# A decode block on one core: value cache loaded as one 32 KB packet per partition, the last quarter of w_down in three pieces, four stores on one semaphore

## The chip, the cores and the metric

The kernel runs on one core of a Trainium2 chip. A core has a matrix engine (TensorE, PE in the profile, with its weight loads shown as PEld), a vector engine (VectorE, DVE), a scalar engine (ScalarE, ACT), a general engine (GpSimd, POOL) and a sync engine (SyncE, SP) that here only issues loads. Sixteen DMA engines move data between the chip's memory (HBM) and the on-chip memory (SBUF, 128 partitions); matmul results go to PSUM, eight banks of 512 float32 per partition. The engines run side by side and wait for one another on semaphores. The metric is the device time of one execution in microseconds; the time before is the median of three runs.

## The reference

One step of a transformer block with conditioning: eight sequences (B = 8), one new token each, a width of 1024, 32 query heads on 4 key/value heads of 128, and a cache of 8192 positions per sequence and head, everything in bfloat16.

```python
mod = (silu(c) @ w_mod).reshape(8, 6, 1, -1)          # sa, ca, ga, sb, cb, gb
h = layernorm(x) * (1 + ca) + sa
q = (h @ wq) as 32 heads of 128
p = softmax(q . k_cache * 128 ** -0.5)                # 8 queries share a key/value head
x = x + ga * ((p . v_cache) @ wo)
h = layernorm(x) * (1 + cb) + sb
gate, up = h @ W_gate, h @ W_up                       # 1024 -> 3584
x = x + gb * ((relu(gate) * up) @ W_down)             # 3584 -> 1024
```

The two caches are 64 MiB each; the weights are some 50 MB. Each byte of them is needed once.

## The kernel before

**Writing order and waits.** Every operation is recorded in one list per engine (`_Graph`); a helper works out which operation must wait for which, and one semaphore per engine counts the operations that somebody waits for. So nearly all instructions carry the line of a helper: 366 for matmuls (`mm`), 370 for transposes on TensorE (`tr`), 374 for VectorE (`dve`), 377 for ScalarE (`act`), 684 for the loads on SP, 87 for the small transfers. The pair loop is emitted as a hardware loop on TensorE, VectorE and ScalarE: one turn is two pairs, and the waits in it are on values that grow with the turn.

**Loads.** All loads go through SP in one order (`stream`, lines 291 to 328), into a ring of five slots of 32 KB per partition, A to E. A load waits until the last user of what lay there before is done (lines 682 to 687). The order is w_mod in two halves, wq in two halves, keys of pair 0, then for each pair n the keys of pair n + 1 and the values of pair n, wo's first half after the values of pair 0, wo's second half, w_gate and w_up in halves, and w_down. Keys alternate between slots A and B, values between C and D. Each key or value load is 4 MiB.

**A pair.** Pair n is one sequence and two of its four key/value heads (16 pairs). The keys come as 128 rows per partition, 32 KB in one piece: partitions 0 to 63 hold the first head's rows, 64 to 127 the second's. The values come in two pieces of 16 KB per partition, one per head, each partition holding 64 rows of each head (line 309).

- `slot_keys(n, j)`, 16 slots per pair: eight 128x128 transposes of keys into one of three PSUM banks taken in turn (`t_bank`), copied out by VectorE (even slots) or ScalarE (odd). Line 507 picks the key rows so that the order of the keys in the scores agrees with that of the values.
- `slot_scores`: for each two slots, four matmuls with a stationary of 32 columns and 512 moving columns, on the four column groups of the array; the scores of a pair fill two banks of 128 partitions.
- `soft_max` to `soft_exp`: the maximum per partition, brought together over partitions with two small matmuls, and one `Exp` on ScalarE that writes P, 128 x 1024, and its row sums.
- `turn_p(n, h)`: P is turned with four 128x128 transposes for each half h, and the copies into `pt` (VectorE for h = 0, ScalarE for h = 1) put the columns in the order in which the values are used.
- `pv(n, u)`, u = 0 to 7: four matmuls, on the four column groups, with 32 columns of `pt` stationary and 512 columns of values moving; all eight steps add up in bank 7 (`W`).
- `pv_evac`, `o_sum`, `o_evac`: the 128 x 512 sums are multiplied with a mask (`diag`) that keeps a quarter of them, summed over four groups, added over partitions with a matmul (`sel`) which also adds the row sums, divided, and put in place for the output projection.

These stages are interleaved over pairs (lines 590 to 628): while slot j of pair n is turned, pair n - 1 gets its maximum (j = 2), exponent (6), turn of P (8) and value products (9 to 15), and pair n - 2 its output (0 to 3).

**Before and after the loop.** POOL fills constants and two identities; VectorE derives masks from them (`spread`, lines 394 to 404) and clears five banks. Then come the transposes of x and silu(c), the products with w_mod, the first layernorm, and q. After the loop: wo, the second layernorm, gate and up, and w_down (lines 659 to 671): four quarters of seven row groups, four matmuls of 256 columns for each. The first two quarters are one load, the third is one, and the last comes as six row groups and one. Two VectorE operations make the output rows; four stores of 4 KB, two on SP and two on ScalarE's queue, each have a semaphore (`osem`), and SP waits for all four at the end.

Of the kernel before, what the change touches and what calls it, by code (L numbers as in the profile page):

```python
# [11 lines left out]
class _Op:  # L12
    __slots__ = ("eng", "fn", "deps", "inc", "value", "idx", "sem", "semval")

    def __init__(self, eng, fn, idx):
        self.eng = eng
        self.fn = fn
        self.deps = []
        self.inc = False
        self.value = 0  # L20
        self.idx = idx
        self.sem = None
        self.semval = 0


# [160 lines left out]
def bass_adaLN_cond__gqa_block_cached__glu_gated_reglu__decode_kernel(  # L186
# [24 lines left out]
    NP = B * G // 2  # L211
# [8 lines left out]
    with ExitStack() as es:  # L220
# [29 lines left out]
        P = sb("P", [128, 1024], bf16)  # L250
        pt = sb("pt", [128, 1024], bf16)
        ov = sb("ov", [128, 512], f32)
        od = sb("od", [128, 132], f32)
        rl = sb("rl", [128, 1], f32)
        tm = sb("tm", [128, 128], f32)
        sel = sb("sel", [128, 128], f32)
        sel16 = sb("sel16", [128, 16], f32)
        diag = sb("diag", [128, 4, 128], bf16)
        blk = sb("blk", [128, 8, 16], f32)
# [17 lines left out]
        xsem = E(nc.semaphore("d_x"))  # L277
        osem = [E(nc.semaphore("d_o%d" % i)) for i in range(4)]

# [73 lines left out]
        loads["v", -1] = loads["wq", 0]  # L353
        place["v", -1] = ring[:, D_:D_ + SLOT].rearrange("p (a n) -> p a n", a=2)

# [37 lines left out]

        def spread(view, n, tile, key):
            dve("tensor_reduce", sel16[:, 0:n], view, AX.X, ALU.add, reads=["identf"], writes=["sel16"])
# [5 lines left out]
        dve("tensor_reduce", sel16[:, 0:4], identf[:].rearrange("p (q i r) -> p i q r", q=4, i=4), AX.XY, ALU.add, reads=["identf"], writes=["sel16"])  # L401
        dve("tensor_copy", diag[:], sel16[:, 0:4, None].to_broadcast([128, 4, 128]), reads=["sel16"], writes=["diag"])
        spread(identf[:].rearrange("p (y k) -> p k y", k=8), 8, blk, "blk")
# [137 lines left out]
        def soft_exp(n):  # L541
            act(P[:].rearrange("p (i k a) -> p i a k", k=64, a=2), S(n).rearrange("p h (i a k) -> p (h i) a k", i=4, a=2), ACT.Exp,
                bias=nb[:], scale=SCALE, accum_out=od[:, 128:129], reads=[pS(n, 0), pS(n, 1), "nb"], writes=["P", "od1"])

        def turn_p(n, h):
            t = t_bank()
            for i in range(4):
                tr(TB(t)[:, 128 * i:128 * (i + 1)], P[:, 512 * h + 128 * i:512 * h + 128 * (i + 1)], identb[:], ["P", "identb"], [pT[t]])
            to = pt[:, 512 * h:512 * (h + 1)].rearrange("p (r i h) -> p i r h", r=16, i=4)
            of_ = TB(t)[:, 0:512].rearrange("p (i r h) -> p i r h", i=4, r=16)  # L550
            if h == 0:
                dve("tensor_copy", to, of_, reads=[pT[t]], writes=[("pt", 0)])
            else:
                act(to, of_, ACT.Copy, reads=[pT[t]], writes=[("pt", 1)])

        def pv(n, u):
            h, jj = u // 4, u % 4
            for q2 in range(2):
                j = 8 * h + 2 * jj + q2
                for gl in range(2):  # L560
                    q = 2 * gl + q2
                    at = 512 * h + 32 * (8 * gl + 4 * q2 + jj)
                    mm(W[32 * q:32 * (q + 1), :], pt[:, at:at + 32],
                       place[("v", n)][:, gl, 512 * j:512 * (j + 1)], u == 0, u == 7, [("pt", h)], [pW], ("v", n))

        def pv_evac(n):
            dve("tensor_tensor", out=ov[:], in0=W, in1=diag[:].rearrange("p i d -> p (i d)"), op=ALU.mult, reads=[pW, "diag"], writes=["ov"])
            dve("tensor_reduce", od[:, 0:128], ov[:].rearrange("p (i d) -> p d i", i=4), AX.X, ALU.add, reads=["ov"], writes=["od"])
# [90 lines left out]
        for c_ in range(4):  # L659
            for i in range(7):  # L660
                if c_ < 2:
                    key, w = ("wd", 0), place[("wd", 0)][:, c_, i, :]
                elif c_ == 2:
                    key, w = ("wd", 1), place[("wd", 1)][:, i, :]
                elif i < 6:
                    key, w = ("wd", 2), place[("wd", 2)][:, i, :]
                else:
                    key, w = ("wd", 3), place[("wd", 3)][:, 0, :]
                for q in range(4):
# [3 lines left out]
        dve("tensor_tensor", out=outR[:], in0=fR, in1=x1R[:], op=ALU.add, reads=["ov", "x1R"], writes=["outR"])  # L673
        last = []
        for q in range(4):
            o = g.dma("sp" if q % 2 == 0 else "act", out.rearrange("b o d -> (b o) d")[:, 256 * q:256 * (q + 1)], outR[32 * q:32 * q + B, :],
                      osem[q], 16, reads=["outR"])
            last.append(o)

# [48 lines left out]
```

## Time and profile before

| | |
|---|---|
| median of three runs | 440.71 us (440.56 to 440.88) |
| the profiled execution | 440.41 us, of which the span of the profile is 438.2 us |
| TensorE busy | 307.3 us, 70% of the span |
| VectorE, ScalarE busy | 184.2 us and 180.5 us, 42% and 41% |
| moved by DMA | 185.81 MB, 424 GB/s over the span |
| granted TensorE clock, mean | 0.895 |

The profile is one execution on the chip. A page gives busy times, queues and the costliest groups; views of the trace give the chain of work that ended last, instructions in order of time with what ended the idle time before them, and busy times by stage. Times are in microseconds from the start of the span unless marked ns. A line of the timeline has the start, the duration from the first to the last of the instructions in it, engine, line, operation, output and inputs, shapes, the count, and in brackets the idle time before it and its releaser. The trace also has a record of every DMA packet, with its start, duration, size and queue, though not its DMA engine; where the text speaks of one engine's packets, these records were strung together by size and time.

### The profile page before, as it was taken

The numbers are of one execution on the slowest core, as the hardware profiler recorded it, in microseconds if no ns is written. First come the engines' busy times: TensorE is split into PE (matmuls) and PEld (weight loads), VectorE is DVE, ScalarE is ACT, GpSimd is POOL, SyncE is SP. The second block draws the span as 40 slices with busy tenths as digits, with TensorE's granted clock in tenths as the row PEclk, the third lists the DMA queues.
The fourth block names the chain that finished last, engine by engine and source line by source line (L and its number), as shares of the span: only waits on it lengthen the run. The fifth ranks groups of instructions, "written<-read, shape, count | busy, mean of one in ns | idle before, by whom it ended". The sixth has DMA issues, their size and how long they took to land.

```text
span 438.2 us, 9770 instructions
## 1 busy us (share of the span) xinstructions
PE 307.3 (70%) x3999; PEld 185.4 (42%) x3999; DVE 184.2 (42%) x358; ACT 180.5 (41%) x197; POOL 9.4 (2%) x48
## 2 busy tenths in 40 slices
PE   1415458896978888696777879677787979656063
PEld 1102135554554655354454545445454655232031
DVE  4102046635372654636264554627355464431010
ACT  3000017463654646464473646456464646300000
POOL 3000000000000000000000000000000000000000
PEclk9968669996999799999999989999998899885666
DMA  8999999999999999999999999999999999999994
GB/s 362 431 431 432 443 432 408 449 429 424 419 450 414 447 419 449 420 438 434 426 438 425 437 425 437 429 431 441 425 440 429 447 416 449 421 429 439 419 431 199
DMA packets 8908, 185.81 MB, mean 424 GB/s; under 512 B 785, under 2 KB 817, under 8 KB 961
## 3 DMA queue, kind: packets, MB, share of 16 engines
q1 hardware_dynamic: 8832, 185.61, 98.6%
q8 instruction: 9, 0.15, 0.1%
q10 hardware_dynamic: 64, 0.04, 0.0%
q14 instruction: 3, 0.02, 0.0%
HBM read 185.63 MB, written 0.02 MB: 424 GB/s over the span
## 4 chain that ended last, share of the span: by engine, by line
DMA 61%; PE 21%; issue 8%; DVE 6%; ACT 2%; DVEq 0%; SPq 0%; ACTq 0%
DMA ring<-in_A_k_cache_dram 45%; PE PS L370 11%; PE PS L366 10%; DMA ring<-in_B_W_up_dram 6%; DMA ring<-in_B_W_down_dram 6%; DMA ring<-in_w_mod_dram 4%; ACT KT L377 2%; DVE KT L374 2%; DVE ov L374 1%; DVE tm L374 1%; DVE nm L374 1%; ACT P L377 0%; DVE nb L374 0%; DVE rl L374 0%; DVEq L161 0%
## 5 line engine op out<-in xcount | busy, mean ns | idle before, releaser
L377 ACT ACTIVATE KT<-PS 128x1024 bf16<-128x1024 bf16 (+1 forms) x132 | 132.9, 1008 | 173.2 <-PE PS L370 85.5
L370 PE MATMUL PS<-identb,ring 128*128 128x128 bf16 x2048 | 159.9, 226 | 27.4 <-DMA ring<-in_A_k_cache_dram 27.4
L370 PEld LDWEIGHTS PS<-identb,ring 128*128 128x128 bf16 x2048 | 122.7, 101 | 83.1 <-issue 66.4
L374 DVE COPY KT<-PS 128x1024 bf16<-128x1024 bf16 (+1 forms) x130 | 89.5, 689 | 162.0 <-PE PS L370 118.9
L366 PE MATMUL PS<-KT,Z 128*32 128x512 bf16 x516 | 53.6, 403 | 0.2 <-ACT KT L377 0.2
L366 PE MATMUL PS<-ring,pt 128*32 128x512 bf16 x544 | 49.6, 384 | 0.2 <-DVE pt L374 0.2
L377 ACT ACT_TABLE_LOAD x11 | 14.1, 1283 | 32.0 <-PE PS L370 30.3
L377 ACT ACTIVATE P<-PS,nb 128x1024 bf16<-128x1024 f32 x17 | 24.0, 1410 | 6.3 <-DVE nb L374 4.8
L366 PE MATMUL PS<-od,sel 128*128 128x129 f32 x36 | 10.2, 369 | 18.2 <-DVE od L374 18.2
L366 PE MATMUL PS<-ring,h2T 128*8 128x512 bf16 (+1 forms) x128 | 11.9, 548 | 13.4 <-DMA ring<-in_B_W_up_dram 9.9
L374 DVE TENSOR_REDUCE mp<-PS 128x1 f32<-128x1024 f32 x17 | 20.6, 1213 | 0.0
L366 PEld LDWEIGHTS PS<-KT,Z 128*32 128x32 bf16 x516 | 13.4, 93 | 14.9 <-issue 1.6
L366 PE MATMUL PS<-ring,siluT 128*8 128x512 bf16 x96 | 9.3, 560 | 14.6 <-DMA ring<-in_w_mod_dram 14.6
L370 PE MATMUL PS<-identb,P 128*128 128x128 bf16 x136 | 13.7, 227 | 7.2 <-ACT KT L377 7.1
L374 DVE TENSOR_REDUCE od<-ov 128x128 f32<-128x512 f32 x18 | 18.4, 1021 | 0.6
L366 PEld LDWEIGHTS PS<-ring,pt 128*32 128x32 bf16 x544 | 14.2, 95 | 7.9 <-issue 0.6
L366 PEld LDWEIGHTS PS<-od,sel 128*128 128x128 f32 x36 | 6.3, 220 | 22.2 <-DVE od L374 22.2
L366 PE MATMUL PS<-ring,hT 128*8 128x512 bf16 x64 | 6.9, 606 | 10.6 <-DMA ring<-in_A_wq_dram 10.6
L377 ACT ACTIVATE pt<-PS 128x512 bf16<-128x512 bf16 x17 | 10.1, 597 | 9.9 <-PE PS L370 9.9
L374 DVE TENSOR_TENSOR ov<-PS,diag 128x512 f32<-128x512 f32 x18 | 12.3, 682 | 3.1 <-PE PS L366 3.1
L370 PEld LDWEIGHTS PS<-identb,P 128*128 128x128 bf16 x136 | 8.0, 100 | 12.5 <-ACT KT L377 9.9
L366 PEld LDWEIGHTS PS<-ring,h2T 128*8 128x8 bf16 x128 | 3.8, 118 | 21.1 <-DMA ring<-in_B_W_up_dram 11.5
(84 smaller groups left out, 128.7 us busy)
## 6 DMA issues: line engine op xcount, KB each, us to landing
ring<-in_A_k_cache_dram SPq DMA_DIRECT2D x16, 4096.0 KB, 22.0
ring<-in_A_v_cache_dram SPq DMA_DIRECT2D x16, 4096.0 KB, 30.8
ring<-in_w_mod_dram SPq DMA_DIRECT2D x2, 6144.0 KB, 24.1
ring<-in_A_wq_dram SPq DMA_DIRECT2D x2, 4096.0 KB, 46.0
ring<-in_A_wo_dram SPq DMA_DIRECT2D x2, 4096.0 KB, 32.3
ring<-in_B_W_gate_dram SPq DMA_DIRECT2D x2, 3584.0 KB, 25.0
ring<-in_B_W_up_dram SPq DMA_DIRECT2D x2, 3584.0 KB, 31.5
ring<-in_B_W_down_dram SPq DMA_DIRECT2D x1, 3584.0 KB, 37.3
```

Source lines behind the costliest of these rows:

```text
L366: return pe(lambda e: e.matmul(out_, lhsT, rhs, start=start, stop=stop, skip_group_check=True), reads, writes, block, deps)
L370: return pe(lambda e: e.matmul(out_, in_, ident, start=True, stop=True, is_transpose=True), reads, writes, block)
L374: return g.op("dve", lambda e: getattr(e, name)(*args, **kw), reads, writes)
L377: return g.op("act", lambda e: e.activation(*args, **kw), reads, writes)
```

## The change

Three parts.

1. **Values.** A value load takes 128 consecutive rows per partition, as the keys do, so that each partition receives 32 KB of one head in one piece. Partitions 0 to 63 hold the first head's rows, 64 to 127 the second's. What follows from it: the keys need no reordering in `slot_keys`, and `soft_exp` writes P in plain order. In `turn_p`, P is turned by 32 transposes of 64x64 for both halves together, the first head's block in partitions 0 to 63 and the second's in 64 to 127, and the result is copied into a `pt` twice as wide in two copies per half, one per head, so that for each head the other head's partitions stay zero (`pt` is filled with zeros on POOL at the start). `pv` has 16 steps of four matmuls of 256 columns instead of 8 steps of four of 512. `pv_evac` works on 256 columns, and `o_sum` uses a new mask `selo` for the output and the old `sel` for the row sums: two matmuls instead of one. A new function `early` moves the waits of the transposes of P onto the operation ahead of them on TensorE, which in the loop is the last key transpose of slot 8.
2. **w_down.** The last quarter comes as four, two and one row groups.
3. **Stores.** The four stores count on one semaphore, and SP waits once, for 64.

```diff
-        osem = [E(nc.semaphore("d_o%d" % i)) for i in range(4)]
+        osem = E(nc.semaphore("d_o"))
...
-            block(("v", n), (C_, D_)[n % 2], SLOT, A_v_cache[b, 2 * gp:2 * gp + 2].rearrange("g (p c) d -> p g (c d)", p=128), (2, 64 * Dh), "v%d" % (n % 2))
+            block(("v", n), (C_, D_)[n % 2], SLOT, A_v_cache[b].rearrange("g s d -> (g s) d")[2 * gp * Sk:2 * (gp + 1) * Sk, :].rearrange("(p c) d -> p c d", p=128),
+                  (128, Dh), "v%d" % (n % 2))
...
-        block(("wd", 2), B_ + 7 * D, 6 * D, wd[:, 3, 0:6], (6, D))
-        block(("wd", 3), B_ + 13 * D, D, wd[:, 3, 6:7], (1, D))
+        block(("wd", 2), B_ + 7 * D, 4 * D, wd[:, 3, 0:4], (4, D))
+        block(("wd", 3), B_ + 11 * D, 2 * D, wd[:, 3, 4:6], (2, D))
+        block(("wd", 4), B_ + 13 * D, D, wd[:, 3, 6:7], (1, D))
...
-                        (Z[:], 0.0, ("Z", 0)), (od[:], 1.0, "od"), (KT[:, 6, :], 0.0, ("KT", 6)), (KT[:, 7, :], 0.0, ("KT", 7))):
+                        (Z[:], 0.0, ("Z", 0)), (pt[:], 0.0, "pt"), (od[:], 1.0, "od"), (KT[:, 6, :], 0.0, ("KT", 6)), (KT[:, 7, :], 0.0, ("KT", 7))):
...
+        spread(identf[:].rearrange("p (q g i h) -> p g h q i", q=4, g=2, i=2), 16, selo, "selo", AX.XY)
+        spread(identf[:].rearrange("p (q i r) -> p i q r", q=8, i=2), 2, diag, "diag", AX.XY)
...
-                cc = 64 * (e_ % 2) + 4 * j + e_ // 2
-                tr(TB(t)[:, 128 * e_:128 * (e_ + 1)], place[("k", n)][:, cc, :], identb[:], ["identb"], [pT[t]], ("k", n))
+                tr(TB(t)[:, 128 * e_:128 * (e_ + 1)], place[("k", n)][:, 8 * j + e_, :], identb[:], ["identb"], [pT[t]], ("k", n))
...
-            act(P[:].rearrange("p (i k a) -> p i a k", k=64, a=2), S(n).rearrange("p h (i a k) -> p (h i) a k", i=4, a=2), ACT.Exp,
+            act(P[:], S(n).rearrange("p h c -> p (h c)"), ACT.Exp,
                 bias=nb[:], scale=SCALE, accum_out=od[:, 128:129], reads=[pS(n, 0), pS(n, 1), "nb"], writes=["P", "od1"])
+
+        def early(at):
+            ops = g.prog["pe"]
+            while ops[at - 1].apart:
+                at -= 1
+            for o in ops[at:]:
+                o.apart = True
+                ops[at - 1].deps.extend(o.deps)
+                o.deps = []
 
         def turn_p(n, h):
             t = t_bank()
-            for i in range(4):
-                tr(TB(t)[:, 128 * i:128 * (i + 1)], P[:, 512 * h + 128 * i:512 * h + 128 * (i + 1)], identb[:], ["P", "identb"], [pT[t]])
...
+            at = len(g.prog["pe"])
+            for i in range(8):
+                for gl in range(2):
+                    r = slice(64 * gl, 64 * (gl + 1))
+                    tr(TB(t)[r, 64 * i:64 * (i + 1)], P[r, 512 * h + 64 * i:512 * h + 64 * (i + 1)], identb[r, r], ["P", "identb"], [pT[t]])
+            if n + 1 < NP:
+                early(at)
+
+            for gl in range(2):
+                r = slice(64 * gl, 64 * (gl + 1))
+                to = pt[r, 1024 * h:1024 * (h + 1)].rearrange("p (x g c) -> p g x c", g=2, c=16)[:, gl]
+                of_ = TB(t)[r, 0:512].rearrange("p (x c) -> p x c", c=16)
+                if h == 0:
+                    dve("tensor_copy", to, of_, reads=[pT[t]], writes=[("pt", h, gl)])
+                else:
+                    act(to, of_, ACT.Copy, reads=[pT[t]], writes=[("pt", h, gl)])
 
         def pv(n, u):
...
+            v = place[("v", n)].rearrange("p (h j q e) d -> p h q e j d", h=2, j=4, q=2)
+            for t in (2 * u, 2 * u + 1):
+                for q in range(4):
+                    at = 32 * (4 * t + q)
+                    mm(W[32 * q:32 * (q + 1), 0:256], pt[:, at:at + 32], v[:, t // 8, q // 2, t % 8, 2 * (q % 2):2 * (q % 2) + 2, :],
+                       t == 0, t == 15, [("pt", t // 8, 0), ("pt", t // 8, 1)], [pW], ("v", n))
 
         def pv_evac(n):
...
+            dve("tensor_tensor", out=ov[:, 0:256], in0=W[:, 0:256], in1=diag[:].rearrange("p i d -> p (i d)"), op=ALU.mult, reads=[pW, "diag"], writes=["ov"])
+            dve("tensor_reduce", od[:, 0:128], ov[:, 0:256].rearrange("p (i d) -> p d i", i=2), AX.X, ALU.add, reads=["ov"], writes=["od"])
 
         def o_sum(n):
-            mm(W[:, 0:129], sel[:], od[:, 0:129], True, True, ["sel", "od", "od1"], [pW])
+            mm(W[:, 0:128], selo[:], od[:, 0:128], True, True, ["selo", "od"], [pW])
+            mm(W[:, 128:129], sel[:], od[:, 128:129], True, True, ["sel", "od1"], [pW])
...
-                for o in last:
-                    e.wait_ge(o.sem, o.semval)
+                e.wait_ge(osem, 64)
```

More of the change, by code (lines that the diff above doesn't have):

```diff
@@ L12 @@
 class _Op:
-    __slots__ = ("eng", "fn", "deps", "inc", "value", "idx", "sem", "semval")
+    __slots__ = ("eng", "fn", "deps", "inc", "value", "idx", "sem", "semval", "apart")
     def __init__(self, eng, fn, idx):
@@ L23, in __init__ @@
         self.semval = 0
+        self.apart = False
 class _Buf:
@@ L250, in bass_adaLN_cond__gqa_block_cached__glu_gated_reglu__decode_kernel @@
         P = sb("P", [128, 1024], bf16)
-        pt = sb("pt", [128, 1024], bf16)
-        ov = sb("ov", [128, 512], f32)
+        pt = sb("pt", [128, 2048], bf16)
+        ov = sb("ov", [128, 256], f32)
         od = sb("od", [128, 132], f32)
@@ L256, in bass_adaLN_cond__gqa_block_cached__glu_gated_reglu__decode_kernel @@
         sel = sb("sel", [128, 128], f32)
+        selo = sb("selo", [128, 128], f32)
         sel16 = sb("sel16", [128, 16], f32)
-        diag = sb("diag", [128, 4, 128], bf16)
+        diag = sb("diag", [128, 2, 128], bf16)
         blk = sb("blk", [128, 8, 16], f32)
@@ L353, in bass_adaLN_cond__gqa_block_cached__glu_gated_reglu__decode_kernel @@
         loads["v", -1] = loads["wq", 0]
-        place["v", -1] = ring[:, D_:D_ + SLOT].rearrange("p (a n) -> p a n", a=2)
+        place["v", -1] = ring[:, D_:D_ + SLOT].rearrange("p (c d) -> p c d", d=Dh)
         def pe(fn, reads=(), writes=(), block=None, deps=()):
@@ L391, in bass_adaLN_cond__gqa_block_cached__glu_gated_reglu__decode_kernel, with spread @@
                                                 pattern=[[-1, 128]], channel_multiplier=1), reads=[k], writes=[k])
-        def spread(view, n, tile, key):
-            dve("tensor_reduce", sel16[:, 0:n], view, AX.X, ALU.add, reads=["identf"], writes=["sel16"])
+        def spread(view, n, tile, key, axes=AX.X):
+            dve("tensor_reduce", sel16[:, 0:n], view, axes, ALU.add, reads=["identf"], writes=["sel16"])
             dve("tensor_copy", tile[:].rearrange("p (a z) -> p a z", a=n) if len(tile.shape) == 2 else tile[:],
@@ L400, in bass_adaLN_cond__gqa_block_cached__glu_gated_reglu__decode_kernel @@
         spread(identf[:].rearrange("p (g y h) -> p g h y", g=2, y=8), 16, sel, "sel")
-        dve("tensor_reduce", sel16[:, 0:4], identf[:].rearrange("p (q i r) -> p i q r", q=4, i=4), AX.XY, ALU.add, reads=["identf"], writes=["sel16"])
-        dve("tensor_copy", diag[:], sel16[:, 0:4, None].to_broadcast([128, 4, 128]), reads=["sel16"], writes=["diag"])
+        spread(identf[:].rearrange("p (q g i h) -> p g h q i", q=4, g=2, i=2), 16, selo, "selo", AX.XY)
+        spread(identf[:].rearrange("p (q i r) -> p i q r", q=8, i=2), 2, diag, "diag", AX.XY)
         spread(identf[:].rearrange("p (y k) -> p k y", k=8), 8, blk, "blk")
@@ L545, in turn_p @@
         def turn_p(n, h):
             t = t_bank()
-            for i in range(4):
-                tr(TB(t)[:, 128 * i:128 * (i + 1)], P[:, 512 * h + 128 * i:512 * h + 128 * (i + 1)], identb[:], ["P", "identb"], [pT[t]])
[L549 to L554, printed above, removed]
@@ L556, in pv @@
-        def pv(n, u):
[L557 to L564, printed above, removed]
+            at = len(g.prog["pe"])
[3 more added lines that the diff above has]
+                    tr(TB(t)[r, 64 * i:64 * (i + 1)], P[r, 512 * h + 64 * i:512 * h + 64 * (i + 1)], identb[r, r], ["P", "identb"], [pT[t]])
@@ L566, in pv_evac @@
+        def pv(n, u):
+            v = place[("v", n)].rearrange("p (h j q e) d -> p h q e j d", h=2, j=4, q=2)
[4 more added lines that the diff above has]
+                       t == 0, t == 15, [("pt", t // 8, 0), ("pt", t // 8, 1)], [pW], ("v", n))
         def pv_evac(n):
-            dve("tensor_tensor", out=ov[:], in0=W, in1=diag[:].rearrange("p i d -> p (i d)"), op=ALU.mult, reads=[pW, "diag"], writes=["ov"])
@@ L568, in pv_evac @@
-            dve("tensor_reduce", od[:, 0:128], ov[:].rearrange("p (i d) -> p d i", i=4), AX.X, ALU.add, reads=["ov"], writes=["od"])
+            dve("tensor_tensor", out=ov[:, 0:256], in0=W[:, 0:256], in1=diag[:].rearrange("p i d -> p (i d)"), op=ALU.mult, reads=[pW, "diag"], writes=["ov"])
+            dve("tensor_reduce", od[:, 0:128], ov[:, 0:256].rearrange("p (i d) -> p d i", i=2), AX.X, ALU.add, reads=["ov"], writes=["od"])
         def o_sum(n):
-            mm(W[:, 0:129], sel[:], od[:, 0:129], True, True, ["sel", "od", "od1"], [pW])
+            mm(W[:, 0:128], selo[:], od[:, 0:128], True, True, ["selo", "od"], [pW])
@@ L664, in bass_adaLN_cond__gqa_block_cached__glu_gated_reglu__decode_kernel @@
                     key, w = ("wd", 1), place[("wd", 1)][:, i, :]
-                elif i < 6:
-                    key, w = ("wd", 2), place[("wd", 2)][:, i, :]
-                else:
-                    key, w = ("wd", 3), place[("wd", 3)][:, 0, :]
+                else:
+                    u = 2 + (i >= 4) + (i >= 6)
+                    key, w = ("wd", u), place[("wd", u)][:, i - (0, 4, 6)[u - 2], :]
                 for q in range(4):
@@ L673, in bass_adaLN_cond__gqa_block_cached__glu_gated_reglu__decode_kernel @@
         dve("tensor_tensor", out=outR[:], in0=fR, in1=x1R[:], op=ALU.add, reads=["ov", "x1R"], writes=["outR"])
-        last = []
         for q in range(4):
-            o = g.dma("sp" if q % 2 == 0 else "act", out.rearrange("b o d -> (b o) d")[:, 256 * q:256 * (q + 1)], outR[32 * q:32 * q + B, :],
-                      osem[q], 16, reads=["outR"])
-            last.append(o)
+            g.dma("sp" if q % 2 == 0 else "act", out.rearrange("b o d -> (b o) d")[:, 256 * q:256 * (q + 1)], outR[32 * q:32 * q + B, :],
+                  osem, 16 * (q + 1), reads=["outR"])
         head = []
```

## The prediction

> **What bounds the kernel now.** I read the queues first, then the stages, then the chain of waits, then the timeline of one pair and of the end. From the page's queues and the table of windows (busy time of PE, PEld, DVE, ACT, POOL; granted clock, DMA share, GB/s):
>
> ```profile
> q1 hardware_dynamic: 8832, 185.61, 98.6%
> q8 instruction: 9, 0.15, 0.1%
> ...
> 97.00:370.60 273.60, 220.97 (x2893) 140.27 (x2894) 138.19 (x253) 149.53 (x161) 4.61 (x27) 0.96 1.01 432
> 370.60:433.20 62.60, 31.65 (x423) 14.84 (x419) 12.77 (x32) 5.56 (x8) 0.51 (x2) 0.71 0.99 424
> 433.20:438.20 5.00, 1.67 (x28) 0.81 (x28) 0.85 (x2) 0.00 (x0) 0.00 (x0) 0.50 0.02 6
> ```
>
> The load queue keeps the 16 DMA engines busy 98.6% of the span, and in the stages up to 433.2 us no compute engine is near its limit. One turn of the loop (two pairs) in the chain of waits:
>
> ```profile
> 198.64 0.63 PE PS L370 x8
> ...
> 215.39 22.00 DMA ring<-in_A_k_cache_dram
> 237.44 0.63 PE PS L370 x8
> ...
> 404.92 28.26 DMA ring<-in_B_W_down_dram
> 433.23 1.69 PE PS L366 x21
> ```
>
> A turn takes 237.44 - 198.64 = 38.80 us. In the trace's packet records, the next packet on the same engine starts 1,209 ns after a 32 KB packet (median of 2,560), 607 ns after a 16 KB packet (4,096) and 6 ns after a semaphore write. A turn has, per engine, 16 packets of 32 KB (keys), 32 of 16 KB (values) and 4 semaphore writes: 19,344 + 19,424 + 24 = 38,792 ns. That is the period: the packets alone set it. The timeline shows the room of TensorE and of the queue:
>
> ```profile
> 196.26 0.60 PE L366 MATMUL PS<-ring,pt 128*32 128x512 bf16 x8
> 198.64 1.07 PE L370 MATMUL PS<-identb,ring 128*128 128x128 bf16 x16 [1.77 <-DMA ring<-in_A_k_cache_dram]
> 201.78 0.49 PE L366 MATMUL PS<-od,sel 128*128 128x129 f32 x2 [1.19 <-DVE od L374]
> 207.74 0.40 PE L370 MATMUL PS<-identb,P 128*128 128x128 bf16 x4
> 208.57 0.40 PE L370 MATMUL PS<-identb,P 128*128 128x128 bf16 x4 [0.44 <-ACT KT L377]
> ...
> 433.23 1.67 PE L366 MATMUL PS<-ring,hmT 128*8 128x256 bf16 x28 [2.67 <-DMA ring<-in_B_W_down_dram]
> 434.95 0.42 DVE L374 TENSOR_TENSOR ov<-PS,gbR 128x256 f32<-128x256 f32 x1 [10.94 <-PE PS L366]
> ```
>
> TensorE ends a pair 1.77 us before the next keys land. If it ran later than that, the key load issued at 215.39 us would be late; but then the engines still hold the rest of a key load and a whole value load, which lands at 227.65 us: 12.3 us of further cover.
>
> **Values in 32 KB packets.** Each value load changes from 16 packets per engine to 8. Two of 607 less one of 1,209 is 5 ns; times 8, times 16 loads: 0.64 us less, all on the path. From below, nothing (the rows are rounded); from above, the packets' own durations, 2 x 611 - 1,213 = 9 ns, 1.15 us. I take 0.64, since starts on an engine are what adds up. The key loads already have this shape and the 1,209 ns. SP issues the same number of value loads.
>
> **w_down.** The six-row piece becomes four and two: 8 more packets per engine and a semaphore write. By a line through 12,288 bytes (456 ns) and 2,048 (80 ns), 8,192 and 4,096 bytes take 306 + 155 = 461 instead of 456 ns, so 8 x 5 + 6 = 0.05 us more. DMA together: -0.59. SP issues one more load of about 0.4 us near 405 us; the pieces land 28 us later, so this and what is behind it on SP are covered. At the end, the six-row piece lands at 433.19 and the last row at 433.82; all 28 matmuls start at 433.23 at about 213 ns per four, the last starts at 434.48, ends at 434.90, and VectorE starts at 434.95. Afterwards the four rows land at about 433.23 - 0.65 - 1.25 = 431.3, two rows at 432.6, the last at 433.82 - 0.59 = 433.23. The 16 matmuls need 0.9 us and the 8 need 0.4, so both are done in time; the last four start at 433.28 and end after 0.37 to 0.42 us (first and later groups of the row above): VectorE at 433.73 instead of 434.95. That is 1.22 less, 0.59 of it counted: 0.63, between 0.5 (a landing 0.1 later) and 0.75 (273 ns matmuls, as the third quarter had at full clock).
>
> **Stores.** SP runs waits at 437.72 and 437.79 us, the branch at 437.86, and drains at 438.01. One wait instead of four can save two steps of 0.07; I take 0.10, bounds 0 and 0.14. The stores themselves are unchanged.
>
> **TensorE, per pair.** (1) Values: 64 matmuls of 256 columns replace 32 of 512. Four column groups run together: 216 ns per four of 512 now, 109 ns per four of 256 in w_down's third quarter at full clock. 16 x 109 against 8 x 216: +0.02; from above, one after another at a transpose's 56 ns, +1.9. The w_down row is nearest, being the same shape but for 8 stationary columns instead of 32. (2) P: 32 half-size transposes replace 8. If the two heads' halves overlap, 16 steps of 56 ns at most: +0.45; none overlapping, 32 x 56: +1.34; half-rate steps: 0. I take +0.45, and +0.18 for two more changes of shape (147 ns instead of 56 between a transpose and a score matmul). (3) Their waits move before the last key transpose of slot 8. This transpose now waits, as the second half of P does today, for ScalarE's slot 7 eviction (to 208.52). The first four transposes of P, 0.22, no longer fit in that wait, and slot 8's own eviction on VectorE, with the pt copies queued behind it, starts about 0.7 later: +0.3, bounds 0 and 1.0. (4) Copies of P into pt: one more of 0.42 us on VectorE and of 0.60 on ScalarE; slot 9's eviction on ScalarE waits behind it, but two slots of TensorE work (1.98 us) exceed ScalarE's 1.02 for two slots. (5) The output: multiply 0.68 to 0.42 (row of 128x256 at the end) and reduce 1.02 to about 0.5 shorten the 1.19 wait for od by 0.75; one more matmul with its weights costs 0.3: -0.45. Sum: +0.5, bounds -0.3 to +4.0, against 1.77 of idle: hidden. Past 1.77 TensorE falls behind, and past 1.77 + 12.3/14 = 2.65 per pair the queue runs dry.
>
> Here the Trainium skill, "TensorEngine Tiling (Array Packing)", Key Properties, speaks against the change: a change of tiling mode drains the array. This trace has only the 147 ns gap; by the rule, with a whole 0.23 us matmul drained at each of two switches, the sum of this part would be 0.3 us larger, still hidden.
>
> **Start.** The memset of pt puts 1.9 us (2 x 0.96, the row of the KT memsets) before the identities on POOL; selo adds 0.65 on VectorE. siluT moves from 10.3 to about 12.9 us; w_mod's first half is awaited until 17.87. Hidden; without that cover it would cost 2.5 us.
>
> **Sum.** -0.59 - 0.63 - 0.10 = -1.32 us. The profiled execution took 440.41 (span 438.2 and 2.2 around it), so 439.09; the median of the runs, 440.71, is 0.30 above it, and I set the forecast against it: 439.4.
>
> **Rivals.** R1, the gain is given back to code loading. Packet records: each 16 KB code block lands on one DMA engine and sets its stream back by about 1.4 us (0.95 + 0.47 at 37.3 us); eight engines were hit once, at 36, 64, 74, 82, 95, 381, 400 and 420 us, and these finish at 433.0 to 433.5, the others at 431.6 to 432.5. TensorE's stream grows by 2 x 58 instructions a pair (232 a turn, about 350 in all), so one more block. If it hits a fresh engine it is free; if an engine that was hit, the end is 1.4 later: 440.8. If instead the packets gain nothing, -0.73 and +0.05 leave 440.0. For R1: an engine can be hit twice; against: eight different ones of eight so far. 0.18 for both, no change.
>
> R2, slower: the loop no longer stays loaded. It has 870 TensorE instructions now (412 weight loads, 412 matmuls, 46 others a turn), 1,102 after. No code packet is seen between 99.5 and 380.8 us, so 870 stay resident. If 1,102 do not, each of 7 returns loads 5 blocks: 35 blocks over 16 engines, 2.2 x 1.4 = 3.1 us: about 442.5, or more if TensorE also stalls. It decides when the buffer is under 1,102 instructions, plus what is fetched ahead. The Trainium skill, "Runtime: NRT & Kernel Launch", Instruction fetch mechanics, gives TensorE 2,048 instructions in 16 KiB blocks, by which this does not happen; it also says a branch out of a two-page window forces a fetch, by which it would. The trace's quiet 281 us contradict that second rule. 0.08.
>
> R3, slower: TensorE becomes the bound, the small matmuls and transposes running one by one. At the upper bounds, +4.0 a pair: 14 x (4.0 - 1.77) - 12.3 = 19 us, 458. For it: no 64-row transpose in the trace; against: the four-group rows. 0.08.
>
> **Numbers.** Forecast 0.66, its own range 439.0 to 440.0 (its extremes, all bounds together, 438.7 and 440.2); R1 0.18, R2 0.08, R3 0.08. A measurement here tells about 0.2%, 0.88 us, from no change. Faster 0.66, same 0.18, slower 0.16. The range, 438.8 to 441.0, holds the forecast and R1.
>
> **What would show it.** Right: a turn of 38.71 to 38.73 us; about 6,900 packets on q1; TensorE still waiting 1 us or more for keys in each pair; about four matmuls behind the last w_down landing and VectorE 0.5 us after it; siluT before w_mod. Wrong: code packets in the middle of the loop (R2); the key wait gone and DMA share below 0.98 there (R3); a last landing at or after 433.8 though the turns are shorter (R1).

## The result, and the profile after

The changed kernel takes 440.15 us (median of 22 runs, 440.00 to 441.07) beside 440.82 us for the kernel before on the same chip (22 runs, 440.53 to 441.81): a ratio of 0.9987, 95% interval 0.9982 to 0.9993. That is 0.67 us less, about half of the 1.32 us that the prediction's sum gave, and less than the 0.2%, 0.88 us, that the prediction took as the least change that can be told from none, though the interval leaves out 1. It lies in the range, but not among the cases called faster, to which the prediction gave 0.66: the range holds it because it was drawn to hold R1 too, and the forecast itself, 439.4, missed by 0.75.

The two profiled executions do not show this sign. That of before, 440.41 us, lies 0.41 under the median of these runs; that of after, 440.72 us (span 438.6), lies 0.57 above its own. So the spans are not compared below, only places in them.

The queues and the table of windows of the changed kernel (start and end; length; busy time of PE, PEld, DVE, ACT and POOL with their instructions; granted clock; DMA share; GB/s):

```profile
q1 hardware_dynamic: 6928, 185.61, 98.3%
q8 instruction: 10, 0.16, 0.1%
...
97.00:370.60 273.60, 225.24 (x3715) 152.79 (x3713) 132.59 (x267) 155.63 (x176) 4.62 (x27) 0.98 1.00 433
370.60:433.20 62.60, 34.59 (x500) 17.95 (x497) 11.75 (x34) 5.88 (x9) 0.51 (x2) 0.70 0.98 418
433.20:438.60 5.40, 2.00 (x28) 0.57 (x28) 0.85 (x2) 0.00 (x0) 0.00 (x0) 0.50 0.04 12
```

The loads have 6,928 packets instead of 8,832. The loop runs at 433 GB/s instead of 432, but the stage behind it at 418 instead of 424, and some of the loads now lie behind 433.2 us (12 GB/s there instead of 6). There is one code packet more. One turn of the loop in the chain of waits, and the chain's last load:

```profile
198.63 1.07 PE PS L374 x16
...
215.19 22.11 DMA ring<-in_A_k_cache_dram
237.34 1.07 PE PS L374 x16
...
404.29 30.09 DMA ring<-in_B_W_down_dram
```

A turn takes 237.34 - 198.63 = 38.71 us instead of 38.80, as forecast (from 137.74 to 331.35 us, five turns of the chain, it is 38.72 on average). So the gain of the packets is there. The load at the end of the chain, now the piece of two row groups, lands 30.09 us after its issue; before's, the piece of six, took 28.26. The end, in the timeline:

```profile
430.03 0.94 PE L370 MATMUL PS<-ring,hmT 128*8 128x256 bf16 x28 [1.09 <-DMA ring<-in_B_W_down_dram]
433.19 1.03 PE L370 MATMUL PS<-ring,hmT 128*8 128x256 bf16 x16 [2.22 <-DMA ring<-in_B_W_down_dram]
434.42 1.00 PE L370 MATMUL PS<-ring,hmT 128*8 128x256 bf16 x12 [0.20 <-DMA ring<-in_B_W_down_dram]
435.03 0.09 PEld L370 LDWEIGHTS PS<-ring,hmT 128*8 128x8 bf16 x4 [0.51 <-DMA ring<-in_B_W_down_dram]
435.47 0.42 DVE L378 TENSOR_TENSOR ov<-PS,gbR 128x256 f32<-128x256 f32 x1 [10.89 <-PE PS L370]
```

The four row groups came at 433.15, the two at 434.37 and the last at 434.99; VectorE starts 0.48 us after the last, instead of 1.12. So the pieces of w_down do what was forecast, on a landing that is later than before's 433.82.

The trace's landing records say why it is late. A load is spread over the 16 DMA engines, and each engine's part counts on the load's semaphore when it has landed, so each load has a first and a last engine. The records do not name the engine: that a block set one back is read from the sixteen landing times of the loads ahead of it and behind it. For the last row group of w_down, in the profiled execution of every run (the distance is taken from times in ns):

| run | first engine landed | last engine landed | apart | code blocks in time to matter | median against before, us |
|---|---|---|---|---|---|
| before | 431.93 | 433.82 | 1.90 | 8 | |
| after | 431.35 | 434.99 | 3.65 | 10 | -0.67 |
| e1_packets | 431.27 | 433.69 | 2.43 | 8 | -0.71 |
| e2_code | 431.87 | 435.70 | 3.83 | 10 | +0.73 |
| e3_tail | 431.85 | 434.36 | 2.52 | 8 | -0.88 |
| e4_pad | 431.86 | 435.16 | 3.31 | 12 | +0.89 |
| e5_small | 431.29 | 434.38 | 3.09 | 9 | -0.27 |
| e6_smaller | 431.54 | 433.61 | 2.07 | 8 | -1.47 |
| e6_again | 431.50 | 433.63 | 2.13 | 8 | -1.45 |
| e7_pad | 431.46 | 434.37 | 2.91 | 9 | -0.61 |

In the changed kernel the first engine lands 0.58 us earlier, as the packets promised (-0.59), and the last one 1.17 us later. The distance between the engines, 2.14 us in the loop (1.90 in before), grew to 3.65 us in two steps, each right behind a code block: with the block at 404.9 us from 2.18 to 3.05, with the one at 429.8 from 2.96 to 3.69. Before had eight blocks that count, at 36, 64, 74, 82, 95, 381, 400 and 420 us (its ninth, at 433.0, came when the loads had all but landed); after has ten, at 36, 65, 75, 83, 90, 97, 380, 392, 405 and 430 us.

### The profile page after: what moved, and what is told of

Same layout as the page of the kernel before. It is cut to its first block, busy times and chain, and to the rows that moved or that the text cites. A ratio compares the mean times of both kernels' runs of the same rounds, so it can differ in the third digit from the quotient of the medians.

```text
span 438.6 us, 11766 instructions
## 1 busy us (share of the span) xinstructions
PE 315.8 (72%) x4987; PEld 202.7 (46%) x4987; DVE 176.8 (40%) x377; ACT 187.4 (43%) x214; POOL 11.2 (3%) x49
## 3 DMA queue, kind: packets, MB, share of 16 engines
q1 hardware_dynamic: 6928, 185.61, 98.3%
## 4 chain that ended last, share of the span: by engine, by line
DMA 55%; PE 27%; issue 7%; DVE 7%; ACT 3%; DVEq 0%; SPq 0%; ACTq 0%; POOLq 0%; POOL 0%
DMA ring<-in_A_k_cache_dram 44%; PE PS L374 14%; PE PS L370 13%; DMA ring<-in_B_W_down_dram 7%; DMA ring<-in_w_mod_dram 4%; DVE KT L378 2%; ACT KT L381 2%; DVE tm L378 1%; DVE nm L378 1%; DVE mp L378 1%; ACT P L381 0%; DVE nb L378 0%; DVE rl L378 0%; DVEq L162 0%; DVE stat L378 0%
## 5 line engine op out<-in xcount | busy, mean ns | idle before, releaser
L374 PE MATMUL PS<-identb,ring 128*128 128x128 bf16 x2048 | 161.3, 225 | 42.2 <-DMA ring<-in_A_k_cache_dram 28.9
L370 PE MATMUL PS<-ring,pt 128*32 128x256 bf16 x1088 | 51.7, 283 | 0.6 <-DVE pt L378 0.6
L370 PEld LDWEIGHTS PS<-ring,pt 128*32 128x32 bf16 x1088 | 24.0, 98 | 13.5 <-issue 0.7
L381 ACT ACTIVATE pt<-PS 64x512 bf16<-64x512 bf16 x34 | 20.1, 591 | 18.7 <-PE PS L374 18.3
L381 ACT ACTIVATE P<-PS,nb 128x1024 bf16<-128x1024 f32 x17 | 18.9, 1114 | 6.8 <-DVE nb L378 5.8
L378 DVE COPY pt<-PS 64x512 bf16<-64x512 bf16 x34 | 14.2, 417 | 4.5 <-PE PS L374 3.9
L370 PE MATMUL PS<-od,selo 128*128 128x128 f32 x36 | 9.8, 358 | 4.8 <-DVE od L378 4.8
L374 PE MATMUL PS<-identb,P 64*64 64x64 bf16 x544 | 12.1, 197 | 0.0
L374 PE MATMUL PS<-identb,KT 8*128 8x8 bf16 (+1 forms) x31 | 2.7, 221 | 12.6 <-DMA KT<-in_A_x_dram 8.7
L370 PEld LDWEIGHTS PS<-ring,siluT 128*8 128x8 bf16 x96 | 2.8, 117 | 19.1 <-DMA ring<-in_w_mod_dram 13.2
L598 POOL CAST ot<-og 128x16 bf16<-128x16 f32 x16 | 4.1, 256 | 295.6 <-DVE og L378 295.6
```

The source lines that it names most:

```text
L370: return pe(lambda e: e.matmul(out_, lhsT, rhs, start=start, stop=stop, skip_group_check=True), reads, writes, block, deps)
L374: return pe(lambda e: e.matmul(out_, in_, ident, start=True, stop=True, is_transpose=True), reads, writes, block)
L378: return g.op("dve", lambda e: getattr(e, name)(*args, **kw), reads, writes)
L381: return g.op("act", lambda e: e.activation(*args, **kw), reads, writes)
L598: pool(lambda e: e.tensor_copy(dst, og[:, n % 2]), reads=[("og", n % 2)], writes=[("ot", n // B)])
```

## The experiments

Each run of a kernel stands beside runs of the kernel before on the same chip: 440.86 us for the first four, 440.84 for e5_small and e6_smaller, 440.91 for the last two. The diff ahead of each is cut to its core.

**e1_packets: the shape of the value loads alone.**

```diff
-            block(("v", n), (C_, D_)[n % 2], SLOT, A_v_cache[b, 2 * gp:2 * gp + 2].rearrange("g (p c) d -> p g (c d)", p=128), (2, 64 * Dh), "v%d" % (n % 2))
+            block(("v", n), (C_, D_)[n % 2], SLOT, A_v_cache[b].rearrange("g s d -> (g s) d")[2 * gp * Sk:2 * (gp + 1) * Sk, :].rearrange("(p c) d -> p c d", p=128),
+                  (128, Dh), "v%d" % (n % 2))
...
```

> Only the shape of the value loads is changed (one 32 KB packet per partition); the computation is that of before and so uses values at the wrong places, which changes no time. Theory A (the packets give their 0.64 us, and the larger code gives part of it back through code blocks that hit a DMA engine twice): turns of 38.71 to 38.73 us, code blocks as before (9), 0.6 us faster than before, ratio 0.9986. Rival B (the slowest DMA engine does not profit from larger packets): turns of 38.80, ratio 1.000.

Measured: 440.15 us (439.92 to 441.30, 11 runs), ratio 0.9987 (0.9978 to 0.9996): -0.71. A turn takes 38.71 to 38.74 us, and the first engine lands at 431.27, 0.66 earlier. So the term for the packets (0.64) is right. In the profiled execution the last engine, at 433.69, is only 0.13 earlier: its engines were 1.05 us apart already at the first load, before any code block, where before's were 0.56 apart. The start differs so from execution to execution (0.56 to 1.11 us in the ten traces), and the medians, not the single landings, say what a change is worth.

**e2_code: the new computation alone, with the old loads and stores.** The diff is against the changed kernel.

```diff
-        osem = E(nc.semaphore("d_o"))
+        osem = [E(nc.semaphore("d_o%d" % i)) for i in range(4)]
...
-            block(("v", n), (C_, D_)[n % 2], SLOT, A_v_cache[b].rearrange("g s d -> (g s) d")[2 * gp * Sk:2 * (gp + 1) * Sk, :].rearrange("(p c) d -> p c d", p=128),
-                  (128, Dh), "v%d" % (n % 2))
+            block(("v", n), (C_, D_)[n % 2], SLOT, A_v_cache[b, 2 * gp:2 * gp + 2].rearrange("g (p c) d -> p g (c d)", p=128), (2, 64 * Dh), "v%d" % (n % 2))
...
-        block(("wd", 2), B_ + 7 * D, 4 * D, wd[:, 3, 0:4], (4, D))
-        block(("wd", 3), B_ + 11 * D, 2 * D, wd[:, 3, 4:6], (2, D))
-        block(("wd", 4), B_ + 13 * D, D, wd[:, 3, 6:7], (1, D))
+        block(("wd", 2), B_ + 7 * D, 6 * D, wd[:, 3, 0:6], (6, D))
+        block(("wd", 3), B_ + 13 * D, D, wd[:, 3, 6:7], (1, D))
...
```

> The changed computation (64x64 transposes, 256-column value products, early waits) with the value loads, w_down pieces and stores of before; values lie at the wrong places, which changes no time. Theory A: turns of 38.80 us, 10 code blocks, engines that are not hit finish as before at about 431.7 us, but the spread between the first and the last engine in the last load grows from 1.9 to 2.5 to 3.5 us; 0 to 1.4 us slower, ratio 1.000 to 1.003. Rival B: spread 1.9 and ratio 1.000. Rival C (the small matmuls and the moved waits lengthen the path): turns over 38.80 us and no wait for keys left.

Measured: 441.59 us (441.40 to 442.24, 11 runs), ratio 1.0017 (1.0008 to 1.0026): +0.73. Its queue of code, from the page, and its end, from the timeline:

```profile
q8 instruction: 10, 0.16, 0.1%
```

```profile
430.57 1.67 PE L368 MATMUL PS<-ring,hmT 128*8 128x256 bf16 x28 [2.10 <-DMA ring<-in_B_W_down_dram]
435.13 1.67 PE L368 MATMUL PS<-ring,hmT 128*8 128x256 bf16 x28 [2.90 <-DMA ring<-in_B_W_down_dram]
436.85 0.42 DVE L376 TENSOR_TENSOR ov<-PS,gbR 128x256 f32<-128x256 f32 x1 [12.48 <-PE PS L368]
```

TensorE waits for the loads in the loop and at the end as in before, a turn takes 38.80 us, and the last piece comes at 435.70 instead of 433.82. VectorE starts 1.15 us behind it, as in before (1.12). So the loss is not the length of TensorE's work. The profiled execution took 442.23 us, 0.64 above the median, and so shows more than the usual loss. The two steps in the landings come with the blocks at 404.3 (2.33 to 3.03) and 430.5 us (2.94 to 3.86).

**e3_tail: w_down's pieces and the one store semaphore alone.**

```diff
-        block(("wd", 2), B_ + 7 * D, 6 * D, wd[:, 3, 0:6], (6, D))
-        block(("wd", 3), B_ + 13 * D, D, wd[:, 3, 6:7], (1, D))
+        block(("wd", 2), B_ + 7 * D, 4 * D, wd[:, 3, 0:4], (4, D))
+        block(("wd", 3), B_ + 11 * D, 2 * D, wd[:, 3, 4:6], (2, D))
+        block(("wd", 4), B_ + 13 * D, D, wd[:, 3, 6:7], (1, D))
...
-        osem = [E(nc.semaphore("d_o%d" % i)) for i in range(4)]
+        osem = E(nc.semaphore("d_o"))
...
```

> Only w_down's pieces of four, two and one and the one store semaphore, on the kernel before. All theories: VectorE starts 0.5 us after the last w_down landing instead of 1.1, SP ends 0.1 earlier after the stores; 0.6 to 0.75 us faster, ratio 0.9984. No change in code blocks or in the spread of 1.9 us beyond chance.

Measured: 439.98 us (439.76 to 440.19, 11 runs), ratio 0.9977 (0.9968 to 0.9986): -0.88, a little more than expected.

```profile
433.76 1.03 PE L367 MATMUL PS<-ring,hmT 128*8 128x256 bf16 x12 [0.22 <-DMA ring<-in_B_W_down_dram]
434.85 0.42 DVE L375 TENSOR_TENSOR ov<-PS,gbR 128x256 f32<-128x256 f32 x1 [10.34 <-PE PS L367]
```

VectorE starts 434.85 - 434.36 = 0.49 us after the last landing. From the end of VectorE's work to the end of the span it is 2.28 us (434.85 + 0.87 to 438.0) and, with four semaphores in before, 2.37: the stores are worth some 0.1 us. The 0.88 is 0.2 above what the parts add up to; the interval, 0.62 to 1.41 us, holds that sum too.

**e4_pad: four code blocks more, nothing else.** The kernel before with 512 tiny matmuls, each with its weight load, put where TensorE waits for the second halves of w_mod and wq.

```diff
+        def idle_code(n):
+            for i in range(n):
+                q = i % 4
+                mm(W[32 * q:32 * q + B, 0:8], identb[:, 0:8], identb[:, 0:8], True, True, ["identb"], [pW])
...
+            if k == 4:
+                idle_code(256)
...
```

> The kernel before with 512 tiny matmuls (1,024 TensorE instructions, four code blocks) where TensorE is idle, waiting for the second halves of w_mod and of wq. Theory A: 13 code blocks, more engines hit twice, spread of the last load 2.5 to 4 us, 0.5 to 1.5 us slower, ratio 1.001 to 1.003. Rival B: the blocks are hidden, ratio 1.000 and spread 1.9. Turns of 38.80 us under both.

Measured: 441.75 us (441.54 to 442.23, 9 runs), ratio 1.0026 (1.0016 to 1.0036): +0.89. Its page:

```profile
q1 hardware_dynamic: 8832, 185.61, 98.3%
q8 instruction: 13, 0.21, 0.2%
```

The 1,024 TensorE instructions brought four packets more on q8, so that queue carries TensorE's code, 256 instructions to a packet.

The first eight blocks (26 to 84 us) each set back another engine. The next four (96, 381, 402 and 423 us) all fell on engines that had been hit already, on four different ones: in the last row group these end 3.0 to 3.3 us behind the first engine, while the eight engines that had met no block end within 0.94 us of it. So the engine does not look drawn at random from 16: the blocks go round eight engines. It would also explain why four blocks more cost no more than one or two.

**e5_small: the changed kernel with a shorter TensorE program.** The diff is against the changed kernel: 277 fewer TensorE instructions (2,375 instead of 2,652 in the program): 1-pass bfloat16 matmuls for small sums that were done in float32 passes, a masked stationary that spreads rows over the four column groups in one matmul, x and silu(c) turned together. The sums so rounded are bfloat16.

```diff
-                for q in range(4):
-                    mm(W[32 * q:32 * q + B, 32 * k:32 * (k + 1)], src[:, k, :], identf[:, 32 * q:32 * (q + 1)], True, True, [skey, "identf"], [pW])
+                mm(W[:, 32 * k:32 * (k + 1)], srcM[:, k].rearrange("p q b -> p (q b)"), foldI[:], True, True, [("KT", 5), "foldI"], [pW])
...
-            mm(W[0:1, 0:128], mp[:], identf[:], True, True, ["mp", "identf"], [pW])
+            mm(W[0:1, 0:128], mp[:], identb[:], True, True, ["mp", "identb"], [pW])
...
```

> The changed kernel with 277 fewer TensorE instructions (2,375 instead of 2,652; before has 2,302): rows made with one masked stationary instead of four, and one-pass bfloat16 instead of two-pass float32 in small matmuls. Theory D (the TensorE code blocks rotate over eight of the sixteen DMA engines, so the ninth and tenth block in the load stream hit an engine a second time): the tenth block disappears, the ninth comes near 431 us; spread of the last landings 2 to 3 us; 439.4 to 440.1 us. Theory A' (blocks hit engines at random): one block fewer than after, 439.9 to 440.2 us. If the code plays no part: as the changed kernel, 440.15.

Measured: 440.57 us (440.13 to 441.03, 11 runs), ratio 0.9991 (0.9982 to 1.0000): a miss, by 0.5 us. The trace shows that it did not get down to eight: a ninth block came at 429.2 us, 2 us before the first engine was done, and fell on an engine that was hit before (its landing went from 1.6 to 3.1 us behind the first). The last landing is at 434.38. The profiled execution, 440.17 us, is 0.40 below the median. The median itself lies 0.42 above the changed kernel's, although one block fewer counts; no trace here shows why, and it stays open.

**e6_smaller: 38 instructions less.** The diff is against e5_small: gate and up in seven chunks of 512 columns instead of eight of 512 and 384, w_down in seven groups of four rows (the last pieces are two, one and one row groups), the first layernorm's sums in bfloat16; 2,337 instructions.

```diff
-                for j, (lo, hi) in enumerate(((0, 512), (512, 896))):
-                    for q in range(4):
-                        mm(bank(b0 + j)[32 * q:32 * q + B, 0:hi - lo], h2T[:, k, :], w[:, 896 * q + lo:896 * q + hi], k == 0, k == KD - 1,
+                for f in range(7):
+                    j, q = f // 4, f % 4
+                    mm(bank(b0 + j)[32 * q:32 * q + B, :], h2T[:, k, :], w[:, 512 * f:512 * (f + 1)], k == 0, k == KD - 1,
...
-        block(("wd", 2), B_ + 7 * D, 4 * D, wd[:, 3, 0:4], (4, D))
-        block(("wd", 3), B_ + 11 * D, 2 * D, wd[:, 3, 4:6], (2, D))
-        block(("wd", 4), B_ + 13 * D, D, wd[:, 3, 6:7], (1, D))
+        block(("wd", 2), B_ + 8 * D, 2 * D, wd[:, 6, 0:2], (2, D))
+        block(("wd", 3), B_ + 10 * D, D, wd[:, 6, 2:3], (1, D))
+        block(("wd", 4), B_ + 11 * D, D, wd[:, 6, 3:4], (1, D))
...
```

> As the kernel before with a further 38 TensorE instructions less (2,337): gate and up in seven chunks of 512 columns instead of eight, w_down's row groups regrouped to match (24 more packets per DMA engine, 0.11 us), layernorm sums in bfloat16. Theory D: the ninth code block comes at 432 us or later, when the load streams are nearly over; no engine is hit twice before 432 us, spread 1.9 to 2.5 us, 439.2 to 439.7 us, below both kernels. Theory A': spread like before and after alike, some double hits, 439.7 to 440.2. If the code plays no part: 440.2.

Measured: 439.37 us (439.31 to 439.67, 5 runs), ratio 0.9963 (0.9949 to 0.9977): the fastest kernel here, 0.8 us under the changed one. Its ninth block came at 432.8 us, when the last row group had landed from eight of the sixteen engines. The page's queue of code, and the end in the timeline:

```profile
q8 instruction: 9, 0.15, 0.1%
```

```profile
433.65 0.39 PE L374 MATMUL PS<-ring,hmT 128*8 128x256 bf16 x4 [0.26 <-DMA ring<-in_B_W_down_dram]
434.09 0.42 DVE L382 TENSOR_TENSOR ov<-PS,gbR 128x256 f32<-128x256 f32 x1 [9.50 <-PE PS L374]
```

Against e5_small the last landing is 434.38 - 433.61 = 0.77 us earlier and the span 0.8 us shorter. But three other edits lie between the two, so the next run puts the block back alone.

**e7_pad: e6_smaller with one code block more.** The diff is against e6_smaller.

```diff
             w = place[("wq", k // 4)][:, k % 4, :]
+            for i in range(128 if k == 4 else 0):
+                mm(W[32 * (i % 4):32 * (i % 4) + B, 0:8], identb[:, 0:8], identb[:, 0:8], True, True, ["identb"], [pW])
```

> The kernel of the run e6_smaller (439.37 us, last w_down landing at 433.61 us, TensorE code blocks at 36, 68, 79, 86, 95, 142, 386, 412 and, too late to matter, 433 us) with exactly one code block more: 128 tiny matmuls with their weight loads (256 TensorE instructions, 16 KB) in the wait for the second half of wq, where TensorE idles; nothing reads what they write, and no load, no other engine and no later instruction changes. Theory D (code blocks rotate over eight DMA engines, so the ninth before the end lands on an engine that was hit before and moves the last landing by up to 1.4 us): nine blocks before 415 us, the ninth near 412 us; spread between the first and the last engine's landing 2.9 to 3.5 instead of 2.07 us; last w_down landing 434.4 to 435.0 us; 440.2 to 440.8 us. Rival (e6_smaller is faster than e5_small and the changed kernel through its other edits, its 512-column chunks and regrouped w_down, and the place of the code blocks does not matter): 439.3 to 439.6 us, last landing at 433.6 us.

Measured: 440.30 us (440.20 to 440.94, 11 runs), ratio 0.9987 (0.9978 to 0.9996); beside e6_again, the same kernel without the block, 440.30 - 439.46 = +0.84 us. The queue of code, and VectorE's start in the timeline:

```profile
q8 instruction: 10, 0.16, 0.1%
```

```profile
434.85 0.42 DVE L382 TENSOR_TENSOR ov<-PS,gbR 128x256 f32<-128x256 f32 x1 [9.62 <-PE PS L374]
```

The ninth block came at 412.2 us and took the engine on which it fell from 1.6 to 3.0 us behind the first, a step of 1.4; the last landing is 434.37 instead of 433.63, while the first engine's, 431.46, is that of e6_again (431.50): the added matmuls did not hold up the loads as a whole. Of a step only what rises above the engine that was slowest until then counts: in this profile the distance went from 2.4 to 2.9 us. So the block's price depends on how far ahead the struck engine was, and the 0.84 us of the medians is a mean over such cases. The rival, by which the other edits made the gain, gave 439.3 to 439.6 and falls.

**e6_again: e6_smaller a second time, beside e7_pad.** The kernel is that of e6_smaller.

> The kernel of e6_smaller once more, on the chip of e7_pad, so that the two can be compared beside the same runs of the kernel before. Both theories: 439.3 to 439.7 us, a last w_down landing within 0.4 us of 433.6 (the first load's skew between engines differs from execution to execution).

Measured: 439.46 us (439.25 to 439.99, 5 runs), ratio 0.9965 (0.9951 to 0.9978).

## Why the prediction was right or wrong

**Values in 32 KB packets: right.** Forecast 0.64 us; the period is 38.71 us, as forecast, and the shape alone gave 0.71. Packets on the load queue: about 6,900 forecast, 6,928.

**w_down: right.** VectorE was to start 0.5 us behind the last landing; it starts 0.48 behind it (1.12 in before). The last matmuls were to be four: the timeline shows the last four weights loaded at 435.03, behind the landing at 434.99 (its row of 12 matmuls joins them with the eight of the two-row piece). e3_tail, which has this and the stores alone, gained 0.88 where -0.05 + 0.63 + 0.10 = 0.68 was forecast for them.

**Stores: right.** 0.10 forecast; from the end of VectorE's work to the end of the span 2.37 us in before and 2.24 in after.

**The sum of DMA time: right for the first engine, wrong for the last.** This is the step that failed. The sum, -0.59 for the DMAs, was made for one engine's stream and taken for the landing of the load, which is that of the slowest engine. The text did see what sets an engine back, 1.4 us for a 16 KB code block, and that the 350 instructions bring one more. It then gave R1 a chance of only 0.18, on the ground that eight blocks had fallen on eight different engines. The profile shows the sign that it had named for R1: shorter turns, and a last landing behind 433.8 us. Two things were wrong in the 0.18. The ninth block of before was left out of the count because it came at 433 us, too late to matter; the longer program pulls it forward to 404.9 us, so two blocks more count, not one. And "eight different ones of eight" was read as a sign that a ninth would find another free engine; the runs show the opposite. In five kernels with nine to twelve blocks (after, e2_code, e4_pad, e5_small, e7_pad), ten blocks came behind the eighth, and all ten fell on an engine that was hit before. So R1 is what happened, at about half its price: its 440.8 us lies 1.4 above the forecast, the median, 440.15, lies 0.75 above it. Two blocks set two engines back by 1.4 to 1.5 us each, and these were not the slowest ones, so the last landing moved by 0.87 and 0.73 us in the profile.

The price of the additional code can be read three ways. e2_code, which has it alone, two blocks more in time: +0.73. One block put into e6_smaller: +0.84. In the whole, -0.67 less the parts without it, -0.71 and -0.88: +0.92. And where the blocks are kept at eight, with the same value packets and stores, e6_smaller takes 439.4 us, the time that the forecast gave to the change. How closely it does so is in part chance, since it also has w_down regrouped, 24 packets per engine more, and other edits that no run parts.

The Trainium skill, "Runtime: NRT & Kernel Launch", Instruction fetch mechanics, says that a crossing of a 16 KiB boundary costs one DMA tail-bump, mostly hidden. The table of waits of the changed kernel puts all idle time of TensorE's matmuls down to loads and other engines, none to code; but in a kernel whose DMA engines are busy 98% of the time the block costs time all the same: 0.84 us for one that falls on an engine already behind. The same section gives TensorE 128 KiB, which is eight such blocks; whether that is why they go round eight engines, no run shows.

**TensorE: hidden, as forecast, but its sum had the wrong sign.** The table of windows for one pair at full clock in both kernels (the rows for 179.40 and 218.10 us, before and then after):

```profile
179.40:198.60 19.20, 15.12 (x206) 9.57 (x206) 9.83 (x18) 11.34 (x12) 0.34 (x2) 1.00 1.01 434
218.10:237.40 19.30, 15.16 (x206) 9.61 (x206) 9.83 (x18) 11.34 (x12) 0.34 (x2) 1.00 1.01 434
```

```profile
179.40:198.60 19.20, 16.87 (x264) 11.68 (x264) 9.54 (x19) 11.74 (x13) 0.33 (x2) 0.91 1.00 430
218.10:237.40 19.30, 15.87 (x265) 10.66 (x266) 9.44 (x19) 11.73 (x13) 0.34 (x2) 1.00 1.01 435
```

The wait for keys that the prediction quoted, 1.77 us at 198.64, is 1.09 at 198.63 in after: by that row alone TensorE would have lost 0.68 us a pair. But the clock granted to that pair was 0.91 in after and 1.00 in before. The pair from 218.1 us has the full clock in both, and there TensorE works 218.16 to 235.67 in before, 17.51 us, and 218.10 to 235.46 in after, 17.36 us: 0.15 less, where +0.5 was forecast (bounds -0.3 to +4.0). Over all pairs TensorE waits 28.9 us for keys, instead of 27.4. Lines of that pair, before and then after:

```profile
218.16 1.06 PE L370 MATMUL PS<-identb,ring 128*128 128x128 bf16 x16 [2.04 <-DMA ring<-in_A_k_cache_dram]
221.31 0.49 PE L366 MATMUL PS<-od,sel 128*128 128x129 f32 x2 [1.20 <-DVE od L374]
...
228.35 0.61 PE L370 MATMUL PS<-identb,ring 128*128 128x128 bf16 x8
```

```profile
218.10 1.06 PE L374 MATMUL PS<-identb,ring 128*128 128x128 bf16 x16 [2.18 <-DMA ring<-in_A_k_cache_dram]
220.39 0.49 PE L370 MATMUL PS<-od,selo 128*128 128x128 f32 x2 [0.34 <-DVE od L378]
...
225.86 0.56 PE L374 MATMUL PS<-identb,ring 128*128 128x128 bf16 x7
227.00 0.23 PE L374 MATMUL PS<-identb,ring 128*128 128x128 bf16 x1 [0.58 <-ACT KT L381]
227.16 0.69 PE L374 MATMUL PS<-identb,P 64*64 64x64 bf16 x32
228.10 0.62 PE L374 MATMUL PS<-identb,ring 128*128 128x128 bf16 x8 [0.25 <-DVE KT L378]
```

Counted from the pair's first key transpose, the output's part ends sooner: the transposes behind it start at 2.75 us instead of 3.48 (-0.73; forecast -0.45, of which the wait fell by 0.86 as against 0.75). Slot 8 starts at 7.76 instead of 8.57 (-0.81), and slot 9 at 10.00 instead of 10.19: the turn of P with its earlier waits costs 0.62, where +0.45, +0.18 and +0.3 were forecast. The value products take 7.36 instead of 7.32 us from there to the end: +0.04 (forecast +0.02). The waiting point was as the text put it: the last key transpose of slot 8 waits 0.58 us for ScalarE's eviction. What made the turn cheap are the small transposes: the two heads' halves do overlap, and 32 take 0.69 us with 0.19 us for one, so a start every (0.69 - 0.19) / 31 = 16 ns, or 32 ns for a step of two, where the forecast had 56 ns for a step, as of those of 128x128. A change of shape cost no more than the forecast allowed: the first small transpose starts 0.16 us behind a key transpose of 0.23 us, before that one has ended by the profile. The Trainium skill, "TensorEngine Tiling (Array Packing)", Key Properties, says that a change of tiling mode drains the array; in this trace that is not seen as a whole matmul's time.

**R2 and R3 fell.** No TensorE code block comes between 97.0 and 380.0 us in after, though a turn of the loop has about 1,100 TensorE instructions. TensorE waits 0.57 to 3.08 us for keys in every pair of the loop. The prediction had named waits of 1 us or more as a sign of being right; two are shorter, 0.57 and 0.98 us, but before has three such, 0.41, 0.49 and 0.99 us.

**Start: right.** siluT is written at 12.57 to 12.76 us (forecast 12.9); TensorE waits for w_mod until 18.09.

## What to carry to other kernels

Where the DMA queues set the time, the instructions of the program are also a load: count the 16 KB blocks that an engine's program fetches before the last data has landed, and add what the slowest DMA engine, not the mean one, has to carry. A change that lengthens a program should be costed with the block that it pulls forward, also where the instructions themselves are hidden; here e6_smaller, with 315 instructions fewer than the changed kernel and w_down regrouped, gained 0.8 us on it, as much as the change itself, while e5_small, with 277 fewer, gained nothing. And a wait read from one pair of each profile is only comparable if the granted clock is.

## What the runs showed that was not expected

- The TensorE code blocks go round eight of the sixteen DMA engines. Each sets its engine back by about 1.4 us; the first eight fell on eight different ones in each of the ten traces, every later one that came in time on an engine that was hit before. By the number of blocks that came in time, the first and last engine end 1.90 to 2.52 us apart with eight blocks, 2.91 and 3.09 with nine, and 3.65 and 3.83 with ten (3.31 with twelve, where the last four fell on four different engines). These are single executions, and those of the two kernels with ten blocks were 0.57 and 0.64 us above their medians.
- The place of the ninth block matters more than the program's length as such: 2,375 instructions brought it at 429.2 us and 2,337 at 432.8 us, and the times are 440.57 and 439.37 us. Other edits lie between these two; e7_pad, with the block put back alone, shows 0.84 us of it.
- `Exp` on ScalarE over 128 x 1024 takes 1.11 us when it writes P in plain order; with the permuted order of before it took 1.41 us (17 each, rows of the page by form). This was no term of the prediction.
